# Second MoE: the second product by seven block products in passes 2 and 3, its weights' parts kept in DRAM

## The chip, the cores and the metric

The kernel runs on one core of a Trainium2 chip. The metric is device time in microseconds (us) from one execution. Before the change the median of 3 runs is 1450.73 us (1449.69 to 1453.21).

## The reference

Attention (4 batches, 8 heads, 576 tokens, head size 64, block-causal mask) gives x, 2304 tokens x 512. A first, gated MoE follows, then the second MoE, which the change is about:

```python
def _moe2_ref(x, domain_probs, w1, w2):      # x 2304x512, w1 4x512x1024, w2 4x1024x512
    p = domain_probs / (domain_probs.sum(-1, keepdims=True) + 1e-09)
    for e in range(E):                       # E = 4
        h = np.maximum(x @ w1[e], 0.0)
        out += p[:, e:e + 1] * (h @ w2[e])
```

All in fp32. On the chip each fp32 operand is split into a high and a low part of the reduced type fp32r, and a product is three matmuls: high x high, high x low, low x high.

## The kernel before, in words

Attention and the first MoE come first; the second MoE begins at about 688 us. It works in three passes (`NPASS`) of 768 tokens. A pass has two token halves t = 0, 1 of `TH` = 384 tokens. The 4 x 1024 hidden units are cut into 16 blocks q of 256, two halves a of 128 each, and taken in pairs (q0, q0+1), 8 pairs a pass.

The first product (`l1_items`) is already done with seven block products in place of eight (Winograd's form of Strassen's scheme): x and W1 are cut 2x2 into blocks, sums of blocks are formed, and seven products m = 1 to 7 are accumulated in the PSUM banks c1, c2 (two buffers each) and c3 (one). A step is one product: 6 matmuls of 128 weights x 384 columns. After a step `snap` (L923, ScalarE) saves a partial sum, or `fin` adds it (L930, VectorE) and makes h: a relu on ScalarE gives the high part (L932), a subtraction on VectorE the low one (L933), in a tile of the ring hb.

The second product (`l2_items`) is plain: for each half t and each tile of 128 tokens one PSUM bank o (three buffers) takes 12 matmuls of 128 weights (h) x 512 columns (W2), over 2 blocks, 2 halves, 3 part pairs. `tok` multiplies the bank by the expert's probability and adds it into acc (L966; L964 for the first pair), which is written out after the last pair.

Weights are loaded and prepared in every pass: `w_load` and `w2_load` on the SP queue; `w_prep` forms four sums of W1 blocks on GpSimd (L875, tile wt) and splits all into high and low parts (ScalarE and VectorE, `split3`, L811 and L814; ring w1g of 5, w1d of 1); `w2_prep` splits W2 (copy on ScalarE, low part on GpSimd, ring w2 of 3).

The order of the work: the items of the first product of a pair, with the preparation of the next pair's weights put between them, are merged by cost with the items of the second product of the pair before (`_merge`). The tile framework then orders each engine's instructions by a simulated time line, takes ready ones first, and sets all waits, so an engine's order may differ from the program's; on the chip each engine keeps that order. Weight preparation of blocks 0 and 1 runs in the last pass of the first MoE.

The first MoE serves as a comparison. Its first product has the same form with 288 columns; its split weights are made once, stored in DRAM (wcd, wod) and loaded again in later passes (L571, L578). Its second product lo writes, in its first two passes, a single PSUM bank: each part is 6 matmuls, and its result is taken out by VectorE (L783) or ScalarE (L781) before the next; 48 parts a pass.

Of the kernel before, what the change touches and what calls it, by code (L numbers as in the profile page):

```python
# [59 lines left out]
def attention_moe_moe_kernel(  # L60
# [467 lines left out]
    def w1_at(f, k):  # L528
        return wc_d[f][:, WAT[k][0] * QF:WAT[k][1] * QF].rearrange("p (h n f) -> p h n f", h=2, f=QF)
# [268 lines left out]
    if True:  # L798
# [39 lines left out]
        def w2_load(q):  # L838
            e, fo = q // QPE, (q % QPE) * QF
            r2 = p2.tile([P, 2, DM], F32, tag="wr2", name="wr2", bufs=2)  # L840
            nc.sync.dma_start(out=r2, in_=w2[e, fo:fo + QF, :].rearrange("(a p) d -> p a d", p=P))
            wq["r2", q] = r2

        def w2_prep(q):
            t = wq[q, "2"] = p2.tile([P, 2, 2, DM], F32R, tag="w2", name="w2", bufs=3)
            split3(t[:, 0], t[:, 1], wq.pop(("r2", q)), "a", "p")

        def w_prep(q):
            r = []
            d = {}  # L850

            def v(t):
                return t.rearrange("p (k f) -> p k f", f=P)

            def b(k, a):
                return d["r1"][:, k, :, a, :]

            def pair(k, src):
                t = wq[q, k] = p2r.tile([P, 2, 2, QF], F32R, tag="w1g", name="w1g", bufs=W1B)
                split3(t[:, 0], t[:, 1], src)  # L860

            def own():
# [4 lines left out]
                split3(t[:, 0].rearrange("p j (k f) -> p (j k) f", f=P),  # L867
                       t[:, 1].rearrange("p j (k f) -> p (j k) f", f=P), src)

            def sums(n):  # L870
                if n == 0:
                    d["t"] = p2r.tile([P, 4, QF], F32, tag="wt", name="wt")
                t = d["t"]
                x, y = [(b(0, 1), b(0, 0)), (b(1, 1), v(t[:, 0])), (b(1, 1), b(0, 1)), (b(1, 0), v(t[:, 1]))][n]
                nc.gpsimd.tensor_tensor(out=v(t[:, n]), in0=x, in1=y, op=ALU.subtract)  # L875

            def last():
                t = wq[q, "d"] = p2r.tile([P, 2, 1, QF], F32R, tag="w1d", name="w1d")
# [20 lines left out]
                nc.vector.tensor_tensor(out=pr_t[:, :, e], in0=pr_t[:, :, e], in1=ps_t, op=ALU.mult)  # L899

        hb = {}

        def l1_items(p, q):

            r = []
            d = {}

            def prod(m, tag, start, bufs):
                if start:
                    d[tag] = ps2.tile([P, 512], F32, tag=tag, name=tag, bufs=bufs)  # L910
                ps = d[tag][:, :TH]
                kind, n = WOP[m]
                w, x = wq[q, kind], xc[m]
                for k in range(KH):
                    ks = slice(k * P, (k + 1) * P)
                    for i, (hw, hx) in enumerate(((0, 0), (0, 1), (1, 0))):
                        mm(("p1", tag), out=ps, lhsT=w[:, hw, n, ks], rhs=x[:, hx, k],
                           start=start and k == 0 and i == 0, stop=k == KH - 1 and i == 2,
                           skip=not start)

            def snap(n):
                t = d[n] = p2.tile([P, TH], F32, tag="snap", name="snap", bufs=4)
# [31 lines left out]
        def l2_items(p, q0):  # L954
# [33 lines left out]
                            r.append((3.0 * 232, lambda t=t, tt=tt, q=q, a=a: part(t, tt, q, a)))  # L988
            return r
# [107 lines left out]
        ps2 = tc.alloc_tile_pool(name="ps2", bufs=1, space=PSUM, reuse_waits="tile")  # L1097
        for q in (0, 1):
            w2_load(q)
        prev = [(0.0, lambda q=q: w2_prep(q)) for q in (0, 1)]  # L1100
        for p in range(NPASS):
            for q0 in range(0, NQ, 2):
                last = p == NPASS - 1 and q0 == NQ - 2
                items = l1_items(p, q0) + l1_items(p, q0 + 1)
                if (p, q0) == (0, 0):
                    m = len(items) // 2
                    items = [items[m * (c == "B") + "1526743".index(x)] for c, x in
                             ("A1", "A2", "A5", "B1", "A6", "B2", "A7", "B6", "B5", "A4", "B7", "A3", "B4", "B3")]
                side = []
                if (p, q0) == (0, 0):  # L1110
                    side += wp[1][-2:]
                if not last:
                    for q in (q0 + 2, q0 + 3):
                        side.append((0.0, lambda q=q: (w_load(q % NQ), w2_load(q % NQ))))
                    for q in (q0 + 2, q0 + 3):
                        side += w_prep(q % NQ) + [(0.0, lambda q=q: w2_prep(q % NQ))]
# [12 lines left out]
        p2.release()  # L1129
# [31 lines left out]
```

## Time and profile before

| | |
|---|---|
| median of 3 runs | 1450.73 us |
| the profiled execution | 1450.08 us |
| its span, first to last instruction | 1448.1 us |
| TensorE matmul busy in the span | 1405.2 us (97%) |
| VectorE, ScalarE, GpSimd busy | 919.7, 785.9, 540.9 us |
| DMA | 229.12 MB |

The profiled execution is one run, taken by the hardware profiler. A busy time counts every moment at which at least one instruction of the engine ran; matmuls overlap, so the busy share of TensorE is not the share of its peak, and the time from one matmul's start to the next is shorter than a matmul's duration.

### The profile page before, as it was taken

The page shows a single profiled execution, that of the slowest core. Times are in us where ns is not written, and L with a number is a line of the kernel's source. Part 1 is how long each engine was busy: PE and PEld are TensorE (multiplying, and loading weights), DVE is VectorE, ACT ScalarE, POOL GpSimd, SP SyncE. Part 2 cuts the span into 40 slices and gives each one's busy share as a digit, 9 for nine tenths or more (in the row PEclk, how much of TensorE's full clock was granted, in tenths as well). Part 3 has the DMA queues.
Part 4 walks back from the last instruction along what each step waited for, and adds up shares of the span by engine and source line. Part 5 has one row for each costly group of instructions (what it writes and reads, how often), then busy time and mean ns, then how long its engine had stood idle before and what let it go on. Part 6 is the DMA issues. An engine that isn't in the chain of part 4 may idle for free. (4 is left out here: it accounts for less than half of the span.)

```text
span 1448.1 us, 23542 instructions
## 1 busy us (share of the span) xinstructions
PE 1405.2 (97%) x8288; PEld 1251.5 (86%) x8288; DVE 919.7 (64%) x1927; ACT 785.9 (54%) x1850; POOL 540.9 (37%) x562
## 2 busy tenths in 40 slices
PE   7988999899999999999999999999999999999998
PEld 3456988789888999999898999889899988899997
DVE  5778888986665546567655555765555576555553
ACT  5889988888776333443444444444444344444431
POOL 5876556631111100121433433453443344343330
PEclk9989999999999999999999999999999999999999
DMA  7797887877667987994312222332122222212201
GB/s 222 245 289 230 239 269 238 277 203 206 198 197 240 297 293 247 342 341 175 130 59 73 61 86 73 105 100 71 61 73 74 73 96 81 73 59 88 73 30 44
DMA packets 171941, 229.12 MB, mean 158 GB/s; under 512 B 70704, under 2 KB 122928, under 8 KB 171824
## 3 DMA queue, kind: packets, MB, share of 16 engines
q1 hardware_dynamic: 170736, 227.36, 48.9%
q8 instruction: 66, 1.08, 0.3%
q14 instruction: 51, 0.42, 0.1%
q10 hardware_dynamic: 1088, 0.26, 0.1%
HBM read 185.11 MB, written 42.47 MB: 157 GB/s over the span
## 5 line engine op out<-in xcount | busy, mean ns | idle before, releaser
L115 PE MATMUL o<-w,hb 128*128 128x512 f32 x1728 | 433.2, 392 | 1.0 <-ACT hb L932 1.0
L115 PEld LDWEIGHTS o<-w,hb 128*128 128x128 f32 x1728 | 321.3, 188 | 55.4 <-ACT hb L932 1.5
L115 PE MATMUL c<-xc,w1g 128*128 128x384 f32 x1728 | 342.1, 338 | 1.5 <-ACT snap L923 1.3
L115 PEld LDWEIGHTS c<-xc,w1g 128*128 128x128 f32 x1728 | 308.6, 188 | 20.8 <-ACT snap L923 2.4
L875 POOL TENSOR_TENSOR wt<-wr 128x256 f32<-128x256 f32 x96 | 90.1, 959 | 429.1 <-DMA wr<-in_moe_w_dram 392.2
L933 DVE SCALAR_TENSOR_TENSOR hb<-c,hb 128x384 fp32r<-128x384 f32 x192 | 138.8, 736 | 26.7 <-ACT hb L932 26.5
L365 POOL TENSOR_SCALAR pt<-pt,nm 128x128 f32<-128x128 f32 (+3 forms) x144 | 92.2, 646 | 170.0 <-DVE nm L362 66.2
L115 PE MATMUL lo<-g,wo 128*128 128x288 f32 x888 | 148.3, 299 | 5.1 <-DVE x L783 4.4
L932 ACT ACTIVATE hb<-c 128x384 fp32r<-128x384 f32 x192 | 96.7, 513 | 71.1 <-DVE c L930 59.7
L115 PEld LDWEIGHTS lo<-g,wo 128*128 128x128 f32 x888 | 126.2, 188 | 9.9 <-DVE x L783 6.6
L814 POOL TENSOR_TENSOR w<-wr,w 128x1024 fp32r<-128x1024 f32 x48 | 116.4, 2442 | 34.2 <-ACT w L811 32.9
L814 DVE TENSOR_TENSOR w1g<-wt,w1g 128x512 fp32r<-128x512 f32 x96 | 70.2, 733 | 88.5 <-ACT w1g L811 88.1
L923 ACT ACTIVATE snap<-c 128x384 f32<-128x384 f32 x144 | 68.3, 489 | 101.4 <-PE c L115 99.4
L811 ACT ACTIVATE w1g<-wt 128x512 fp32r<-128x512 f32 x96 | 60.6, 631 | 113.1 <-PE c L115 104.1
L966 DVE SCALAR_TENSOR_TENSOR acc<-o,pr_t,acc 128x512 f32<-128x512 f32 x126 | 92.2, 745 | 34.9 <-PE o L115 34.8
L930 DVE TENSOR_TENSOR c<-c,snap 128x384 f32<-128x384 f32 x144 | 77.1, 552 | 56.0 <-ACT snap L923 51.9
L814 DVE TENSOR_TENSOR w1g<-wr,w1g 128x512 fp32r<-128x512 f32 x48 | 37.2, 774 | 91.0 <-ACT w1g L811 91.0
L115 PE MATMUL c<-xc,wa 128*128 128x288 f32 x504 | 83.0, 300 | 2.9 <-DVE nm L361 1.8
L783 DVE TENSOR_TENSOR x<-lo,x 128x288 f32<-128x288 f32 x124 | 55.6, 452 | 42.7 <-PE lo L115 41.7
L115 PEld LDWEIGHTS c<-xc,wa 128*128 128x128 f32 x504 | 71.2, 189 | 7.1 <-DVE nm L361 2.0
L875 POOL TENSOR_TENSOR wt<-wr,wt 128x256 f32<-128x256 f32 x96 | 74.6, 777 | 3.2
L811 ACT ACTIVATE w1g<-wr 128x512 fp32r<-128x512 f32 x48 | 30.3, 630 | 80.8 <-DMA wr<-in_moe_w_dram 79.2
(142 smaller groups left out, 2435.2 us busy)
## 6 DMA issues: line engine op xcount, KB each, us to landing
wr<-in_moe_w_dram SPq DMA_DIRECT2D x96, 512.0 KB, 3.5
wa<-wcd SPq DMA_DIRECT2D x40, 512.0 KB, 5.1
wb<-wcd SPq DMA_DIRECT2D x40, 512.0 KB, 5.6
wc<-wcd SPq DMA_DIRECT2D x40, 512.0 KB, 4.3
wo<-wod SPq DMA_DIRECT2D x36, 512.0 KB, 6.4
wd<-wcd SPq DMA_DIRECT2D x40, 256.0 KB, 4.6
raw<-in_moe_w_gate_dram SPq DMA_DIRECT2D x12, 512.0 KB, 5.1
raw<-in_moe_w_val_dram SPq DMA_DIRECT2D x12, 512.0 KB, 5.5
```

Of the source, the lines that this page charges most:

```text
L115: ins = nc.tensor.matmul(out=out, lhsT=lhsT, rhs=rhs, start=start, stop=stop, skip_group_check=skip)
L365: nc.gpsimd.tensor_scalar(out=p, in0=p, scalar1=nm[:, 2 + x:3 + x], scalar2=1.0, op0=ALU.mult, op1=ALU.mult)
L783: nc.vector.tensor_tensor(out=x2[t, dm], in0=ps, in1=x2[t, dm], op=ALU.add)
L811: nc.scalar.activation(out=hi, in_=src, func=AF.Copy)
L814: (nc.vector if eng_lo == "v" else nc.gpsimd).tensor_tensor(out=lo, in0=src, in1=hi.bitcast(F32), op=ALU.subtract)
L875: nc.gpsimd.tensor_tensor(out=v(t[:, n]), in0=x, in1=y, op=ALU.subtract)
L923: nc.scalar.activation(out=t, in_=d["c1"][:, :TH], func=AF.Copy)
L930: nc.vector.tensor_tensor(out=c, in0=d[tag][:, :TH], in1=d[n], op=ALU.add)
L932: nc.scalar.activation(out=t[:, 0], in_=c, func=AF.Relu)
L933: nc.vector.scalar_tensor_tensor(out=t[:, 1], in0=c, scalar=0.0, in1=t[:, 0].bitcast(F32), op0=ALU.max, op1=ALU.subtract)
L966: nc.vector.scalar_tensor_tensor(out=acc[tt, t], in0=ps, scalar=prs["t"][:, ti, e:e + 1], in1=acc[tt, t], op0=ALU.mult, op1=ALU.add)
```

## The change

In passes 2 and 3 (index 1 and 2, `FIRSTP` = 1) the second product too is done by seven block products: h is cut into (token half, hidden half), W2 into (hidden half, output half). For each of seven products m and each of three tiles of 128 tokens, `part` makes 6 matmuls of 256 columns (two blocks q, three part pairs), and after each the half bank is added into one or two halves of acc. Nine half banks are placed in five banks (`slot`): three of tag o, two uses of c3.

For that h is kept as fp32 blocks (hf), four sums of blocks are made on GpSimd (`h_sum`), and seven operands are split (`h_split`). W2's seven split operands, sums among them, are made in pass 1 (`w2_prep`, `w2_sums`) and stored in DRAM (`w2_keep`), as W1's split parts are (`keep`); passes 2 and 3 load them (`w1_get`, `w2_get`) and prepare no weights. Pass 1 itself still computes the plain second product. The rings hb and w2 grow from 14 to 19 and from 3 to 4; hf and the sums of h use the rings wr1 and wr2.

```diff
-HB = 14
+HB = 19
+W2B = 4
+FIRSTP = 1
+        w1_d = [dram.tile([P, 14 * QF], F32, name=f"w1d{i}") for i in range(NQ)]
+        w2_d = [dram.tile([P, 7, 2, 2, QF], F32, name=f"w2d{i}") for i in range(NQ // 2)]
+        M2 = (1, 6, 2, 5, 7, 4, 3)
+        def w2_keep(q, m, t):
+            nc.sync.dma_start(out=w2_d[q // 2][:, M2.index(m), :, q % 2], in_=t.bitcast(F32))
         def w2_prep(q):
-            t = wq[q, "2"] = p2.tile([P, 2, 2, DM], F32R, tag="w2", name="w2", bufs=3)
-            split3(t[:, 0], t[:, 1], wq.pop(("r2", q)), "a", "p")
+            r = wq.pop(("r2", q))
+            t = wq[q, "2"] = p2.tile([P, 2, 2, DM], F32R, tag="w2", name="w2", bufs=W2B)
+            split3(t[:, 0], t[:, 1], r, "a", "p")
+            for m, a, n in ((1, 0, 0), (2, 1, 0), (3, 1, 1)):
+                w2_keep(q, m, t[:, :, a, n * QF:(n + 1) * QF])
+            wq["r2t", q] = r
+        def w2_sums(q):
+            r = wq.pop(("r2t", q))
+            s = p2r.tile([P, 4, QF], F32, tag="wt", name="wt")
...
+            for n, (x, y) in enumerate(((b(0, 1), b(0, 0)), (b(1, 1), s[:, 0]), (b(1, 1), b(0, 1)), (b(1, 0), s[:, 1]))):
+                nc.gpsimd.tensor_tensor(out=s[:, n], in0=x, in1=y, op=ALU.subtract)
+            t = p2.tile([P, 2, 4, QF], F32R, tag="w2", name="w2t", bufs=W2B)
+            split3(t[:, 0], t[:, 1], s, "a", "v")
+            for n, m in enumerate((5, 6, 7, 4)):
+                w2_keep(q, m, t[:, :, n])
+        def w2_get(q0, n):
+            k = min(2, 7 - 2 * n)
+            t = p2.tile([P, 2, 2, 2, QF], F32R, tag="w2", name="w2s", bufs=W2B)
+            nc.sync.dma_start(out=t[:, :k].bitcast(F32), in_=w2_d[q0 // 2][:, 2 * n:2 * n + k])
...
+        def w1_get(q):
+            for k in "abcd":
+                n = 1 if k == "d" else 2
+                t = wq[q, k] = p2r.tile([P, 2, n, QF], F32R, tag="w1d" if n == 1 else "w1g", name="w1g", bufs=1 if n == 1 else W1B)
+                nc.sync.dma_start(out=t.bitcast(F32), in_=w1_at(q, k))
+            def keep(k):
+                nc.sync.dma_start(out=w1_at(q, k), in_=wq[q, k].bitcast(F32))
...
+        def h_split(q, m, src, low=None):
+            t = hb[q, m] = p2.tile([P, 2, TH], F32R, tag="hb", name="hb", bufs=HB)
+            nc.scalar.activation(out=t[:, 0], in_=src, func=AF.Copy if low is None else AF.Relu)
+            if low is None:
+                nc.vector.tensor_tensor(out=t[:, 1], in0=src, in1=t[:, 0].bitcast(F32), op=ALU.subtract)
+            else:
+                nc.vector.scalar_tensor_tensor(
+                    out=t[:, 1], in0=src, scalar=0.0, in1=t[:, 0].bitcast(F32), op0=ALU.max, op1=ALU.subtract)
+        def h_sum(q, n, x, y, op):
...
+            nc.gpsimd.tensor_tensor(out=o, in0=x, in1=y, op=op)
+            h_split(q, {1: 5, 2: 6, 3: 7, 4: 3}[n], o)
+        def h_block(q, blk, c):
...
+            nc.scalar.activation(out=hf[q, blk], in_=c, func=AF.Relu)
+            if blk != (1, 0):
+                h_split(q, {(0, 0): 1, (0, 1): 2, (1, 1): 4}[blk], c, True)
+            if blk == (1, 0):
+                h_sum(q, 1, hf[q, (1, 0)], hf[q, (1, 1)], ALU.add)
+                h_sum(q, 2, hf[q, "s", 1], hf[q, (0, 0)], ALU.subtract)
+                h_sum(q, 3, hf[q, (0, 0)], hf[q, (1, 0)], ALU.subtract)
+            if blk == (0, 1):
+                h_sum(q, 4, hf[q, (0, 1)], hf[q, "s", 2], ALU.subtract)
+        def l2s_items(p, q0, nxt):
...
+            def slot(key, tt):
+                n, h = {("c1", 0): (0, 0), ("c1", 1): (0, 1), ("c1", 2): (1, 0), ("c2", 2): (1, 1),
+                        ("c2", 0): (2, 0), ("c2", 1): (2, 1), ("m", 0): (3, 0), ("m", 1): (3, 1), ("m", 2): (4, 0)}[key, tt]
...
+                    tag = "o" if n < 3 else "c3"
...
+            key = {1: "c1", 6: "c1", 7: "c1", 4: "c1", 2: "m", 5: "c2", 3: "c2"}
+            ADDS = {1: ((0, 0),), 2: ((0, 0),), 6: ((0, 1),), 7: ((1, 1),), 5: ((1, 1),), 4: ((1, 0),), 3: ((0, 1),)}
...
+            for x, m in enumerate(M2):
+                for tt in range(NTK):
+                    r.append((6.0 * 121, lambda m=m, tt=tt: step(m, tt)))
+                if nxt is not None and (x % 2 or x == 6):
+                    r.append((0.0, lambda x=x: w2_get(nxt, x // 2)))
...
-        prev = [(0.0, lambda q=q: w2_prep(q)) for q in (0, 1)]
+        prev = []
...
+                    else:
+                        side += [(0.0, lambda q=q: w1_get(q % NQ)) for q in (q0 + 2, q0 + 3)]
...
-                prev = l2_items(p, q0)
+                if p < FIRSTP:
+                    prev = l2_items(p, q0)
+                    if (p, q0) == (FIRSTP - 1, NQ - 2):
+                        prev += [(0.0, lambda n=n: w2_get(0, n)) for n in range(4)]
+                else:
+                    prev = l2s_items(p, q0, None if last else (q0 + 2) % NQ)
```

## Rows read from the trace of the kernel before

**Rows 1.** First line of the page: span and instructions.

```profile
span 1448.1 us, 23542 instructions
```

**Rows 2.** Stretches, about passes 1 and 2: length, busy times (instructions), clock, DMA share, GB/s.

```profile
core 0: us, PE busy (x) PEld busy (x) DVE busy (x) ACT busy (x) POOL busy (x), PEclk, DMA share, GB/s
720.00:971.00 251.00, 249.84 (x1247) 225.50 (x1246) 147.21 (x236) 111.35 (x206) 102.11 (x88) 1.00 0.25 80
971.00:1221.00 250.00, 249.81 (x1246) 225.21 (x1246) 149.74 (x238) 111.33 (x206) 99.04 (x86) 1.00 0.24 76
```

**Rows 3.** Longest wait of TensorE, 760 to 1430 us: total us, times, longest.

```profile
PE o L115 <- ACT hb L932: 1.0, 1, 1.0
```

**Rows 4.** Timeline, unbroken runs of matmuls: start us, length us, ..., count.

```profile
683.84 4.53 PE L115 MATMUL lo<-g,wo 128*128 128x288 f32 x33
688.21 7.55 PE L115 MATMUL c<-xc,w1g 128*128 128x384 f32 x42
1431.76 12.41 PE L115 MATMUL o<-w,hb 128*128 128x512 f32 x54
```

**Rows 5.** Page, costliest groups, whole run: count | busy us, mean ns | idle before.

```profile
L115 PE MATMUL o<-w,hb 128*128 128x512 f32 x1728 | 433.2, 392 | 1.0 <-ACT hb L932 1.0
L115 PE MATMUL c<-xc,w1g 128*128 128x384 f32 x1728 | 342.1, 338 | 1.5 <-ACT snap L923 1.3
L875 POOL TENSOR_TENSOR wt<-wr 128x256 f32<-128x256 f32 x96 | 90.1, 959 | 429.1 <-DMA wr<-in_moe_w_dram 392.2
L933 DVE SCALAR_TENSOR_TENSOR hb<-c,hb 128x384 fp32r<-128x384 f32 x192 | 138.8, 736 | 26.7 <-ACT hb L932 26.5
L115 PE MATMUL lo<-g,wo 128*128 128x288 f32 x888 | 148.3, 299 | 5.1 <-DVE x L783 4.4
L814 DVE TENSOR_TENSOR w1g<-wt,w1g 128x512 fp32r<-128x512 f32 x96 | 70.2, 733 | 88.5 <-ACT w1g L811 88.1
L966 DVE SCALAR_TENSOR_TENSOR acc<-o,pr_t,acc 128x512 f32<-128x512 f32 x126 | 92.2, 745 | 34.9 <-PE o L115 34.8
L930 DVE TENSOR_TENSOR c<-c,snap 128x384 f32<-128x384 f32 x144 | 77.1, 552 | 56.0 <-ACT snap L923 51.9
L783 DVE TENSOR_TENSOR x<-lo,x 128x288 f32<-128x288 f32 x124 | 55.6, 452 | 42.7 <-PE lo L115 41.7
```

**Rows 6.** First MoE, passes 1 and 2: stretches, a wait of TensorE, the adds behind lo.

```profile
149.00:341.00 192.00, 182.21 (x1309) 161.16 (x1308) 163.21 (x427) 164.41 (x457) 101.93 (x119) 1.00 0.79 247
341.00:448.00 107.00, 106.95 (x787) 95.39 (x786) 68.29 (x201) 82.43 (x234) 17.38 (x30) 1.00 0.61 182
...
PE lo L115 <- DVE x L783: 3.3, 4, 1.6
...
L783 DVE TENSOR_TENSOR x<-lo,x 128x288 f32<-128x288 f32 x40 | 18.0, 450 | 2.6 <-PE lo L115 2.2
```

**Rows 7.** Groups by line, 971 to 1221 us: a sum on GpSimd, the subtraction behind one.

```profile
L129 DVE TENSOR_TENSOR xc<-xs,xc 128x384 fp32r<-128x384 f32 x8 | 6.0, 747 | 3.5 <-ACT xc L127 3.4
L617 POOL TENSOR_TENSOR xs<-xr 128x384 f32<-128x384 f32 x2 | 2.6, 1276 | 4.6 <-issue 4.6
```

**Rows 8.** Timeline, 1016 to 1024 us: W2's split, what runs beside it.

```profile
1016.27 1.07 ACT L811 ACTIVATE w<-wr 128x1024 fp32r<-128x1024 f32 x1 [0.54 <-PE o L115]
...
1017.43 2.27 PE L115 MATMUL c<-xc,w1g 128*128 128x384 f32 x12
...
1018.57 4.76 POOL L814 TENSOR_TENSOR w<-wr,w 128x1024 fp32r<-128x1024 f32 x2
...
1021.12 2.63 DVE L933 SCALAR_TENSOR_TENSOR hb<-c,hb 128x384 fp32r<-128x384 f32 x1 [0.59 <-ACT hb L932]
```

**Rows 9.** DMA queue of 704:960, 110:300, 590:680 (packets, MB, share); then a stretch.

```profile
q1 hardware_dynamic: 15729, 21.25, 26.2%
...
q1 hardware_dynamic: 40556, 46.96, 78.4%
...
q1 hardware_dynamic: 12982, 26.82, 84.4%
...
448.00:485.00 37.00, 35.41 (x261) 34.43 (x260) 25.82 (x43) 21.07 (x44) 12.10 (x8) 1.00 0.93 313
```

More of the change, by code (lines that the diff above doesn't have):

```diff
@@ L842, in w2_load, with b, w1_at @@
             wq["r2", q] = r2
+        M2 = (1, 6, 2, 5, 7, 4, 3)
+        def w2_keep(q, m, t):
+            nc.sync.dma_start(out=w2_d[q // 2][:, M2.index(m), :, q % 2], in_=t.bitcast(F32))
         def w2_prep(q):
[L845 to L846 removed]
+            r = wq.pop(("r2", q))
[7 more added lines that the diff above has]
+            s = p2r.tile([P, 4, QF], F32, tag="wt", name="wt")
+            def b(a, n):
+                return r[:, a, n * QF:(n + 1) * QF]
+            for n, (x, y) in enumerate(((b(0, 1), b(0, 0)), (b(1, 1), s[:, 0]), (b(1, 1), b(0, 1)), (b(1, 0), s[:, 1]))):
[8 more added lines that the diff above has]
+            nc.sync.dma_start(out=t[:, :k].bitcast(F32), in_=w2_d[q0 // 2][:, 2 * n:2 * n + k])
+            for x in range(k):
+                wq[q0, "2", M2[2 * n + x]] = t[:, x]
+        def w1_get(q):
[3 more added lines that the diff above has]
+                nc.sync.dma_start(out=t.bitcast(F32), in_=w1_at(q, k))
+        def w1_at(q, k):
+            return w1_d[q][:, WAT[k][0] * QF:WAT[k][1] * QF].rearrange("p (h n f) -> p h n f", h=2, f=QF)
         def w_prep(q):
@@ L901, in attention_moe_moe_kernel @@
         hb = {}
+        hf = {}
+        def h_split(q, m, src, low=None):
[7 more added lines that the diff above has]
+        def h_sum(q, n, x, y, op):
+            if n in (1, 3):
+                hf[q, "u", n] = p2.tile([P, 2, DM], F32, tag="wr2", name="hs", bufs=2).rearrange("p a d -> p (a d)")
+            o = hf[q, "s", n] = hf[q, "u", n - (n + 1) % 2][:, (n + 1) % 2 * TH:((n + 1) % 2 + 1) * TH]
+            nc.gpsimd.tensor_tensor(out=o, in0=x, in1=y, op=op)
+            h_split(q, {1: 5, 2: 6, 3: 7, 4: 3}[n], o)
+        def h_block(q, blk, c):
+            t, a = blk
+            if a == t:
+                hf[q, "t", t] = p2r.tile([P, NKT, QF], F32, tag="wr1", name="hf", bufs=2).rearrange("p a d -> p (a d)")
+            hf[q, blk] = hf[q, "t", t][:, a * TH:(a + 1) * TH]
+            nc.scalar.activation(out=hf[q, blk], in_=c, func=AF.Relu)
[7 more added lines that the diff above has]
+                h_sum(q, 4, hf[q, (0, 1)], hf[q, "s", 2], ALU.subtract)
         def l1_items(p, q):
@@ L988, in l2_items, with add, done, part @@
                             r.append((3.0 * 232, lambda t=t, tt=tt, q=q, a=a: part(t, tt, q, a)))
+            return r
+        begun = set()
+        def l2s_items(p, q0, nxt):
+            r = []
+            e = q0 // QPE
+            NTK = TH // P
+            bank = {}
+            opened = {}
+            def slot(key, tt):
+                n, h = {("c1", 0): (0, 0), ("c1", 1): (0, 1), ("c1", 2): (1, 0), ("c2", 2): (1, 1),
+                        ("c2", 0): (2, 0), ("c2", 1): (2, 1), ("m", 0): (3, 0), ("m", 1): (3, 1), ("m", 2): (4, 0)}[key, tt]
+                new = n not in bank
+                if new:
+                    tag = "o" if n < 3 else "c3"
+                    bank[n] = ps2.tile([P, 512], F32, tag=tag, name=tag, bufs=3 if n < 3 else 1)
+                return bank[n][:, h * QF:(h + 1) * QF], new, n
+            def add(t, n, tt, ps):
+                ti = (p * TP + t * TH) // P + tt
+                pr = prs["t"][:, ti, e:e + 1]
+                if q0 == 0 and (p, tt, t) not in begun:
+                    begun.add((p, tt, t))
+                    acc[tt, t] = p2.tile([P, DM], F32, tag=f"acc{t}{tt}", name="acc")
+                o = acc[tt, t][:, n * QF:(n + 1) * QF]
+                if q0 == 0 and (p, tt, t, n) not in begun:
+                    begun.add((p, tt, t, n))
+                    nc.vector.tensor_scalar(out=o, in0=ps, scalar1=pr, scalar2=None, op0=ALU.mult)
+                else:
+                    nc.vector.scalar_tensor_tensor(out=o, in0=ps, scalar=pr, in1=o, op0=ALU.mult, op1=ALU.add)
+            def done(t, tt):
+                if q0 + 2 == NQ:
+                    ti = (p * TP + t * TH) // P + tt
+                    nc.sync.dma_start(out=out[ti * P:(ti + 1) * P, :], in_=acc[tt, t])
+            key = {1: "c1", 6: "c1", 7: "c1", 4: "c1", 2: "m", 5: "c2", 3: "c2"}
+            ADDS = {1: ((0, 0),), 2: ((0, 0),), 6: ((0, 1),), 7: ((1, 1),), 5: ((1, 1),), 4: ((1, 0),), 3: ((0, 1),)}
+            def part(m, tt):
+                k = key[m]
+                ps, new, n = slot(k, tt)
+                ts_ = slice(tt * P, (tt + 1) * P)
+                for x, q in enumerate((q0, q0 + 1)):
+                    h, w = hb[q, m], wq[q0, "2", m]
+                    for i, (hh, hw) in enumerate(((0, 0), (0, 1), (1, 0))):
+                        first = x == 0 and i == 0
+                        if first and m in (1, 2, 5) and not new:
+                            last_mm["p2", k, tt] = opened[n]
+                        mm(("p2", k, tt), out=ps, lhsT=h[:, hh, ts_], rhs=w[:, hw, x],
+                           start=first and new, stop=x == 1 and i == 2, skip=not new)
+                        if first and new:
+                            opened[n] = last_mm["p2", k, tt]
+                return ps
+            def step(m, tt):
+                ps = part(m, tt)
+                for t, n in ADDS[m]:
+                    add(t, n, tt, ps)
+                if m == 4:
+                    done(1, tt)
+                if m == 3:
+                    done(0, tt)
+            for x, m in enumerate(M2):
[3 more added lines that the diff above has]
+                    r.append((0.0, lambda x=x: w2_get(nxt, x // 2)))
@@ L1111, in attention_moe_moe_kernel @@
                     side += wp[1][-2:]
+                if (p, q0) == (0, 0):
+                    for q in (0, 1):
+                        side += [(0.0, lambda q=q: w2_prep(q)), (0.0, lambda q=q: w2_sums(q))]
                 if not last:
[L1113 to L1116, printed above, removed]
+                    if p < FIRSTP and q0 + 2 < NQ:
+                        for q in (q0 + 2, q0 + 3):
+                            side.append((0.0, lambda q=q: (w_load(q % NQ), w2_load(q % NQ))))
+                        for q in (q0 + 2, q0 + 3):
+                            side += w_prep(q % NQ) + [(0.0, lambda q=q: w2_prep(q % NQ)), (0.0, lambda q=q: w2_sums(q))]
+                    else:
+                        side += [(0.0, lambda q=q: w1_get(q % NQ)) for q in (q0 + 2, q0 + 3)]
                 n = len(items)
```

7 lines of the change are left out of this document (added).

## Prediction

> **What bounds the kernel now.** I read the page first, then the busy times stretch by stretch. The profiled execution took 1450.08 us, of which the span is 1448.1 [rows 1]; the median of the runs shown is 1450.73, so a time worked out against the profiled one needs 0.65 added, which is below what I can resolve. The change lies in the second MoE, which runs from 688 us to the end. There TensorE has next to no gap: in passes 1 and 2 it is busy 249.8 of 251 and of 250 us, at the full granted clock, while VectorE is at 59 to 60%, ScalarE at 44%, GpSimd at 40% and the DMA engines at 24 to 25% [rows 2]. From 760 to 1430 us its longest wait behind another engine is 1.0 us in all [rows 3]. So a pass lasts as long as its matmuls take to issue, and the question is what a matmul costs. A pair of weight blocks (q0, q0+1) has 84 matmuls of the first product (14 steps of 6, 384 columns) and 72 of the second (512 columns), 156 in all; the 1246 instructions of pass 2 are eight pairs, 31.25 us each [rows 2].
>
> The rate of issue is read from unbroken runs, less the last one's duration. 288 columns: (4.53 - 0.30)/32 = 0.132 us. 384: (7.55 - 0.34)/41 = 0.176. 512: (12.41 - 0.39)/53 = 0.227 [rows 4, 5]. Check: 84 x 0.1759 + 72 x 0.2268 = 14.78 + 16.33 = 31.1 us a pair, against 31.25 seen.
>
> **The change, part by part.**
>
> *The second product, passes 2 and 3* (16 pairs). Out go 16 x 72 = 1152 matmuls of 512 columns: 1152 x 0.2268 = 261.3 us. In come 16 x 7 products x 3 token tiles x 2 blocks x 3 = 2016 of 256 columns. No unbroken run of 256 columns with full weights is in the trace. Above, one costs no more than a 288-column one, 0.132 us; below, no less than half a 512-column one, 0.1134 (a fixed part can't be negative). So the product costs 229 to 266 us: from 33 us won to 5 us lost. At 2.4 GHz the columns alone take 0.120, 0.160 and 0.213 us, so the three rows leave 12, 16 and 13 ns of fixed cost; with 13 ns a 256-column matmul takes 0.120 us. The nearest row, 288 columns, less 32 columns gives 0.119. I take 0.120: 2016 x 0.120 = 241.9 us, **19.4 us won**, 1.2 us a pair.
>
> The Trainium skill speaks against short matmuls here: "TensorE: Matmul & The Clock Gate" has a weight load of 128 columns at about 107 ns (section "LDWEIGHTS (loading the stationary operand)") and says that it overlaps a running matmul only in another row group (section "The mechanism"). By it a 512-column matmul would issue every 213 + 107 = 320 ns and a 256-column one every 214, and the change would lose 2016 x 0.214 - 1152 x 0.320 = 63 us. The 0.227 us row disagrees: of such a load only 13 ns shows; the measurement decides.
>
> *Handing banks to VectorE.* Today a pair ends 6 accumulations in one of three o banks, each 12 matmuls (2.7 us) long. After, 21 parts of 6 matmuls (0.72 us) each need an add before TensorE may go on in that place; the parts share five banks, and the third product takes the c3 bank twice a pair, which the first product uses too. That is 16 x 21 = 336 handovers. The nearest rows are those of the first MoE, where the product lo lives in a single bank and each part is 6 matmuls: in its first pass, with VectorE 85% busy (163.21 of 192 us), 48 such parts cost 3.3 us of waiting, 0.07 us each; in its second pass, with VectorE at 64%, TensorE is busy 106.95 of 107 us [rows 6]. So 0 to 23 us. VectorE's load per pair: out go 6 adds (4.5 us), the weight splits (2 x 3.5 x 0.733 = 5.1) and 8 hb subtractions (5.9), in come 21 adds of 256 columns, 6 hb subtractions (4.4) and 8 subtractions behind a GpSimd sum (8 x 0.747 = 6.0) [rows 5, 7]. A 256-column add: L783 and L930, the same operation at 288 and 384 columns, differ by 100 ns, 1.04 ns a column; 745 - 256 x 1.04 = 0.48 us, 10.1 for 21. Net +5.0: from 18.7 to 23.7 us of 30, 79%, between the two rows. But lo's parts follow one another in one bank, while here two thirds have another bank's part between them, and 14 first-product steps a pair can be put in the gaps. I take 0.02 us: **6.7 us lost**.
>
> The Trainium skill ("PSUM — Partial Sum Buffer", section "PSUM bank collisions raise a hardware error") wants a bank guarded whole, not by address. No row here shows two accumulations in one bank. By it the second token tile of a product can't start before the add of the first is done, as they share a bank (rival 3).
>
> *h in blocks.* Per pair ScalarE gets 22 passes over 128x384 for 8, and loses ten weight copies: about even at 44%, nothing on the path. GpSimd gets 8 sums of at most 1.28 us (10.2 us) [rows 7] and loses all weight work (8 sums near 0.87, two splits of 2.4: 11.8 us) [rows 5, 8]. A split of 2.4 us can hold up VectorE's subtraction for as long: L933 took 2.63 us beside one [rows 8]; that pause shortens to 1.3. The chain relu, sum, sum, copy, subtract (some 4.5 us) makes product 6 ready later than hb today; the next pair's first product covers it, 14.8 us that needs none of it. Nothing, except in the last pair.
>
> *Loads in passes 2 and 3.* A pair reads two sets of split W1 (1.84 MB each) and 3.67 MB of split W2: 7.3 MB in 30 us, 245 GB/s, where it was 76. The first MoE moved 298 GB/s from 590 to 680 us at 84% of the engines [rows 9]. All are issued on SP; behind one that waits for its buffer the other loads stand. They have half a pair (15 us) or more in hand. I cost it at nothing; uncovered, a 1 MB load at that rate is 3.5 us a pair, 56 in all.
>
> *Pass 1.* Here W2's sums and all parts are made and stored. Per pair GpSimd gets 8 sums (7 us, to 63%), ScalarE 2 copies of 1.07 us, VectorE 2 subtractions near 1.5 us: all beside TensorE's 31.25 us. The DMA is the tight part. Stored are 14 x 1.84 MB of W1 (the first two blocks mostly before 700 us) and 16 x 1.84 of W2: 55 MB; loads of 14 blocks, 14.7 MB; the two W1 sets for pass 2, 3.7; x and output, 3.2. 77 MB in 251 us is 306 GB/s. While engines are busy they move 21.25/(0.262 x 256) = 317 GB/s in this pass today, 315 from 110 to 300 us, where much is stores, 353 from 590 to 680 [rows 9]: 87 to 97% of the pass. From 448 to 485 us they were at 93% and TensorE lost 1.6 of 37 us [rows 9]; all of that for 251 us would be 10.8, the 84% stretch gives 0. I take **3 us lost**; worst at the 247 GB/s of 149 to 341 us [rows 6]: 77/0.247 = 312 us, 61 lost.
>
> W2's split now waits for the end of the second product with only 4 buffers, two of them for the sums. Before, both splits waited for it too, and TensorE issued 12 first-product matmuls meanwhile [rows 8]; the same covers it here.
>
> *Pass 1 to 2, and the end.* The first four loads of kept W2 follow the last old product: some 5 us behind first-product steps, 0.5 lost. At the end, 54 x 0.2268 = 12.2 us of second product came after the last first-product matmul [rows 4]; now, if 27 of 126 can go ahead, 99 x 0.120 = 11.9, with handovers that nothing fills: 1 lost. **1.5 lost.**
>
> Sum: 1450.1 - 19.4 + 6.7 + 3 + 1.5 = **1442 us**.
>
> **Rivals.**
> 1. *All handovers hidden*, as in the first MoE's second pass, and the stores too: 1450.1 - 19.4 - 0 = 1431. For it: the first product's steps as filler. Against: VectorE fuller.
> 2. *Pass 1 becomes a DMA pass* (the slower side). Stores fill the engines, the weight loads land late behind them on the same queue, and TensorE waits for W1. It decides when pass 1 grows by more than the other 11 us won: below 77/(0.251 + 0.011) = 294 GB/s. At 277 GB/s, between the 298 and the 247 seen, 27 us more: 1442 - 3 + 27 = 1466. For it: no stretch of 90 us moved over 298 here. Against: none was asked to.
> 3. *Adds set the pace of the second product*: a third of the parts, 7 a pair, follow a part in their own bank; where 0.48 us of add is never filled that is 16 x 7 x 0.48 = 54 us, at half 27: 1442 - 6.7 + 27 = 1462. For it: VectorE at 79%; against: fillers.
> 4. *A wash*: handovers at 0.04 us (13 us), pass 1 at 5: about 1450.
>
> **Numbers.** Forecast 0.40, rival 1 0.17, rival 2 0.17, rival 3 0.09, rival 4 0.17. 0.3% (4.4 us) is about what a measurement of this kernel tells from no change: faster 0.57, same 0.17, slower 0.26. The forecast's own range is 1436 to 1446. Range 1428 to 1463: it takes in 0.119 us a matmul with nothing lost, and rival 3.
>
> **What would show it.** Second-product runs of 256 columns at 0.120 us; passes 2 and 3 near 241 us each against 250; waits of the second product behind the adds of about 7 us; pass 1 near 254 us with the DMA share above 0.85. I am wrong if those runs issue at over 0.130, if waits behind adds pass 20 us, or if pass 1 passes 265 us.

## The result, and the profile after

| | before | after |
|---|---|---|
| median of 5 runs | 1450.73 us (1448.90 to 1453.68) | 1429.70 us (1427.74 to 1432.97) |
| ratio of after to before | | 0.9854, 95% interval 0.9832 to 0.9876 |
| the profiled execution | 1450.08 us | 1431.91 us |
| first matmul of the second MoE | 688.2 us | 692.1 us |
| from there to the last matmul of the plain second product of pass 1 | 261.6 us | 262.3 us |
| from there to the end (passes 2 and 3) | 498.3 us | 475.6 us |

The kernel is 21.0 us faster; 1442 was forecast, with 1428 to 1463 as range. So the sign was right and the size less than half of what came; the time is that of rival 1 (1431). The stages, read from the starts of matmuls in the two traces: pass 1 cost 0.7 us, passes 2 and 3 won 22.6. The 3.9 us by which the second MoE starts later lie in the part that wasn't changed; a later profile of the same kernel (e12) starts it at 688.1. Without that part the second MoE takes 759.9 us in the trace before and 738.0 in the trace after.

The first line of the page of the kernel after:

```profile
span 1430.1 us, 26340 instructions
```

The view of stretches of the kernel after, against [rows 2] (columns as there):

```profile
720.00:971.00 251.00, 248.68 (x1252) 225.64 (x1253) 167.73 (x246) 120.34 (x220) 137.34 (x139) 1.00 0.90 311
971.00:1221.00 250.00, 249.40 (x1763) 248.61 (x1762) 180.14 (x361) 113.46 (x251) 79.85 (x75) 1.00 0.71 252
```

TensorE has still no gap to speak of, now with 1763 instructions in 250 us. The matmuls got shorter, not the gaps smaller. VectorE went from 60 to 72% in pass 2, not to the 79% reckoned; the DMA engines are 90% busy in pass 1 and move 311 GB/s.

An unbroken run of the second product in the timeline of the kernel after (start, length, count):

```profile
1408.34 5.07 PE L117 MATMUL o<-w2s,hb 128*128 128x256 f32 x41
```

The groups by line of the kernel after, from 971 to 1221 us (busy, mean ns), to set beside [rows 4, 5, 7]:

```profile
L117 PE MATMUL o<-w2s,hb 128*128 128x256 f32 x909 | 130.0, 282 | 0.5 <-DVE acc L1106 0.5
L1106 DVE SCALAR_TENSOR_TENSOR acc<-o,pr_t,acc 128x256 f32<-128x256 f32 x133 | 62.3, 478 | 28.4 <-PE o L117 26.7
L957 DVE TENSOR_TENSOR hb<-hs,hb 128x384 fp32r<-128x384 f32 x68 | 45.6, 687 | 2.5 <-ACT hb L955 2.4
L959 DVE SCALAR_TENSOR_TENSOR hb<-c,hb 128x384 fp32r<-128x384 f32 x51 | 29.8, 584 | 5.7 <-ACT hb L955 5.5
```

(5.07 - 0.28)/40 = 0.120 us from start to start: the forecast value. The add takes 0.478 us (0.48 forecast).

The view of waits of the kernel after has two lines for TensorE from 965 us on (total us, times, longest); the handovers to VectorE cost 1.1 us, not 6.7:

```profile
PE c L117 <- DMA w1g<-w1d: 1.5, 1, 1.5
PE o L117 <- DVE acc L1106: 1.1, 2, 0.6
```

From start to start these two waits behind an add cost 1.4 us: the view leaves out the end of the running matmuls. Each part has one add, into one half of acc (not "one or two"). How the handovers come to cost so little is seen in the timeline of pass 2 (start, length; TensorE's matmuls and the adds alone):

```profile
1064.37 0.87 PE L117 MATMUL o<-w2s,hb 128*128 128x256 f32 x6
1065.07 1.04 PE L117 MATMUL c<-xc,w1g 128*128 128x384 f32 x5
1065.28 0.48 DVE L1106 SCALAR_TENSOR_TENSOR acc<-o,pr_t,acc 128x256 f32<-128x256 f32 x1 [0.57 <-PE o L117]
1065.95 0.87 PE L117 MATMUL c<-w2s,hb 128*128 128x256 f32 x6
1066.66 1.04 PE L117 MATMUL c<-xc,w1g 128*128 128x384 f32 x5
1066.86 0.48 DVE L1106 SCALAR_TENSOR_TENSOR acc<-c,pr_t,acc 128x256 f32<-128x256 f32 x1 [0.64 <-PE c L117]
1067.54 0.87 PE L117 MATMUL o<-w2s,hb 128*128 128x256 f32 x6
1068.25 0.51 PE L117 MATMUL c<-xc,w1g 128*128 128x384 f32 x2
```

Behind each part of 6 matmuls stand 5 matmuls of the first product, 0.88 us from start to start; the add runs beneath them (1065.28 to 1065.76) and is done before the next part starts. The framework's order mixes the products by single matmuls, not by steps of 6.

### The profile page after: what moved, and what is told of

Same layout as the page of the kernel before. It is cut to its first block, busy times and chain, and to the rows that moved or that the text cites. A ratio compares the mean times of both kernels' runs of the same rounds, so it can differ in the third digit from the quotient of the medians.

```text
span 1430.1 us, 26340 instructions
## 1 busy us (share of the span) xinstructions
PE 1381.3 (97%) x9152; PEld 1276.4 (89%) x9152; DVE 995.2 (70%) x2151; ACT 791.6 (55%) x1930; POOL 546.6 (38%) x594
## 4 chain that ended last, share of the span: by engine, by line
PE 77%; DVE 6%; DMA 6%; ACT 5%; POOL 3%; issue 3%; SPq 1%; DVEq 0%; ACTq 0%; POOLq 0%
PE c L117 34%; PE o L117 24%; PE lo L117 6%; PE s L117 4%; PE obank L117 3%; PE t L117 2%; DMA raw<-in_moe_w_gate_dram 1%; PE tbank L389 1%; DMA raw<-in_moe_w_out_dram 1%; PE s L308 1%; ACT pt L339 1%; DVE raw L508 1%; DMA wr<-in_moe_w_dram 1%; DVE nm L337 1%; DMA w1g<-w1d 1%
## 5 line engine op out<-in xcount | busy, mean ns | idle before, releaser
L117 PE MATMUL o<-w2s,hb 128*128 128x256 f32 x1728 | 243.5, 282 | 1.1 <-DVE acc L1106 1.1
L117 PEld LDWEIGHTS o<-w2s,hb 128*128 128x128 f32 x1728 | 231.8, 189 | 2.0 <-DVE acc L1106 1.7
L966 POOL TENSOR_TENSOR hs<-hf 128x384 f32<-128x384 f32 x64 | 64.1, 1023 | 287.4 <-ACT hf L974 256.3
L1106 DVE SCALAR_TENSOR_TENSOR acc<-o,pr_t,acc 128x256 f32<-128x256 f32 x264 | 123.4, 478 | 57.8 <-PE o L117 55.3
L117 PE MATMUL o<-w,hb 128*128 128x512 f32 x576 | 142.6, 392 | 1.8 <-ACT hb L1016 1.2
L974 ACT ACTIVATE hf<-c 128x384 f32<-128x384 f32 x128 | 65.7, 513 | 116.1 <-DVE c L1011 58.4
L117 PEld LDWEIGHTS o<-w,hb 128*128 128x128 f32 x576 | 107.1, 188 | 21.8 <-ACT hb L1016 1.9
L957 DVE TENSOR_TENSOR hb<-hs,hb 128x384 fp32r<-128x384 f32 x128 | 87.0, 694 | 5.5 <-ACT hb L955 5.3
L117 PE MATMUL c<-xc,wc 128*128 128x288 f32 x432 | 72.2, 302 | 1.8 <-ACT snap L709 1.7
L339 ACT ACTIVATE pt<-s,nm 128x128 f32<-128x128 f32 (+3 forms) x128 | 67.5, 529 | 9.5 <-DVE nm L337 4.9
```

The lines of the kernel that those rows point to most:

```text
L117: ins = nc.tensor.matmul(out=out, lhsT=lhsT, rhs=rhs, start=start, stop=stop, skip_group_check=skip)
L339: nc.scalar.activation(out=pt[:, x * nk:(x + 1) * nk], in_=sp[:, x - x0], func=AF.Exp, bias=nm[:, x:x + 1], scale=1.0, accum_out=nm[:, 2 + ...
L957: nc.vector.tensor_tensor(out=t[:, 1], in0=src, in1=t[:, 0].bitcast(F32), op=ALU.subtract)
L966: nc.gpsimd.tensor_tensor(out=o, in0=x, in1=y, op=op)
L974: nc.scalar.activation(out=hf[q, blk], in_=c, func=AF.Relu)
L1106: nc.vector.scalar_tensor_tensor(out=o, in0=ps, scalar=pr, in1=o, op0=ALU.mult, op1=ALU.add)
```

## The experiments

Theory A: the second product costs the issue of its matmuls, and the handovers are free because the framework's order fills them. Theory B: they are free in any order. Theory C: part of the gain is relief of the other engines from weight work. Theory D: pass 1 stayed under the limit of the DMA, but close to it. Against A stood the prediction's rival 3 (VectorE sets the price). Times are medians, of 8 runs for e1 and e11, of 4 for e2, e9 and e12, of 2 for the others; where a time is set against "before", that is the kernel before on the same chip.

**e1: W1 kept alone.** The second product plain in every pass; only W1's parts are kept, and W2 is loaded and split in every pass.

```diff
+SECOND = 3
-                if p >= FIRSTP:
+                if p >= SECOND:
...
-                if p < FIRSTP:
+                if p < SECOND:
```

> W1's split parts are kept in DRAM and loaded in passes 2 and 3, as after the change; the second product stays plain in all passes, W2 is loaded and split in every pass. Theory A (only the number and length of the second product's matmuls matters): the same matmuls as before, so 1450 us, within 3. Theory C (part of the gain is relief: no weight sums and fewer splits on VectorE, ScalarE and GpSimd in passes 2 and 3): VectorE and GpSimd get 5 and 7 us a pair lighter, and 3 to 10 us of the 21 come already here: 1441 to 1447.

Measured 1446.46 us against 1451.24, ratio 0.998 (0.9963 to 0.9998): 0.3 to 5.4 us faster. In the same stretches as [rows 2] TensorE is busy without a gap:

```profile
720.00:971.00 251.00, 251.00 (x1255) 227.01 (x1254) 139.16 (x225) 104.42 (x194) 87.90 (x72) 1.00 0.55 190
971.00:1221.00 250.00, 250.00 (x1251) 226.13 (x1250) 110.58 (x174) 77.40 (x142) 44.80 (x22) 1.00 0.50 160
```

With the same matmuls 8 and 5 more fit into the two stretches, some 1.6 and 1.0 us. So a small part of the gain comes without the block products, a term the prediction had at nothing; C calls it relief, but e1 also has the larger rings hb and w2, and no run parts the two.

**e2: the block products in pass 3 alone** (as e1 with `SECOND = 2`, all stores of the change in pass 1).

> The block products only in pass 3; pass 2 has the plain second product with W1 from DRAM and W2 split anew; pass 1 as after the change (all stores). Theory A: 8 of the 16 pairs, half of the 22.6 us that passes 2 and 3 won: 11 us less than before, 1439 to 1440. If pass 1's stores or the step from one pass to the next carry a price, or the gain sits in one of the passes, it is away from half by 3 us or more.

Measured 1439.86 us, 11.4 less than before: half, as A says. The interval (9 to 14 us less) leaves room for some 2 us: beyond that, pass 1's stores and the step between passes carry no price of their own.

**e4: the parts together.** From pass 2 on each matmul is tied behind the one before it in the program's order, and the parts follow three first-product steps.

```diff
+        if fixed["on"]:
+            if fixed["last"] is not None:
+                tc.add_manual_dep(ins.ins, fixed["last"].ins.name, NOSYNC, reason="in the order given")
+            fixed["last"] = ins
...
-                _merge(items, prev)
+                fixed["on"] = p >= FIRSTP
+                if p > FIRSTP or (p == FIRSTP and q0):
...
+                    run(items[:steps[2] + 1] + prev + items[steps[2] + 1:])
```

> From pass 2 on TensorE keeps the order as written, and a pair's 21 parts of the second product stand together behind three steps of the first product, so no first-product matmul stands between two parts. Theory A (the handovers to VectorE cost nothing because first-product matmuls fill them): the 7 parts a pair that follow a part in their own bank wait for an add, 0.48 us and two signals, some 0.7 us each, 16 x 7 x 0.7 = 78 us: about 1505, waits of TensorE behind the adds of 60 us or more. Theory B (no filler is needed, the parts in other banks and a quick add are enough): under 10 us of waits, 1430 to 1440.

Measured 1650.67 us. The view of waits of this kernel, TensorE's longest from 965 us on:

```profile
PE o L118 <- DVE acc L1111: 66.7, 88, 2.9
PE c L118 <- ACT snap L1009: 48.0, 60, 1.5
PE c L118 <- DVE acc L1111: 18.5, 32, 0.6
PE o L118 <- DVE acc L1109: 5.7, 8, 1.2
```

A stretch of its timeline (matmuls and adds alone):

```profile
1107.71 0.97 PE L118 MATMUL c<-w2s,hb 128*128 128x256 f32 x6 [0.58 <-DVE acc L1111]
1108.73 0.48 DVE L1111 SCALAR_TENSOR_TENSOR acc<-c,pr_t,acc 128x256 f32<-128x256 f32 x1 [1.07 <-PE c L118]
1109.27 0.98 PE L118 MATMUL c<-w2s,hb 128*128 128x256 f32 x6 [0.58 <-DVE acc L1111]
```

128 waits behind adds, 8 a pair. A part that waits starts 1.56 us after the one before it (1107.71, 1109.27) in place of 0.72: a handover with nothing in the gap costs 0.84 us, of which the view of waits shows 0.58; the rest is the end of the running matmuls and the start of the next. That is 128 x 0.84 = 107 us (112 when every such gap of the trace is added up, since some are longer), and the waits of the first product behind its snap come on top, 58 us counted in the same way, since it has lost its filler too. Some 36 us of the 221 lie in gaps too short for the view. B falls. My 1505 counted the second product's waits alone.

**e5: whole steps, merged as the program has them** (e4's tie, `_merge` kept).

> From pass 2 on TensorE keeps the order in which the program merges the two products (a step of the first product, one or two parts of the second, and so on), in place of the order made by the framework, which mixes single matmuls. Theory A in its strict form (the fine mixing is needed): one gap in three between parts has no filler and a third of these are in one bank, 2 to 3 waits of 0.7 us a pair, 16 x 2.5 x 0.7 = 28 us: about 1457. If whole steps are filler enough: 1430 to 1435. Theory B: 1430 to 1435.

Measured 1577.07 us: both figures missed, in A's direction. The view of waits of this kernel, TensorE's from 965 us on:

```profile
PE o L118 <- DVE acc L1111: 77.0, 88, 3.9
PE c L118 <- DVE acc L1111: 14.1, 17, 0.9
PE o L118 <- DVE acc L1109: 10.0, 8, 4.3
```

A stretch of its timeline (matmuls and adds alone):

```profile
1105.49 0.87 PE L118 MATMUL o<-w2s,hb 128*128 128x256 f32 x6
1106.40 0.48 DVE L1111 SCALAR_TENSOR_TENSOR acc<-o,pr_t,acc 128x256 f32<-128x256 f32 x1 [0.42 <-PE o L118]
1106.93 0.99 PE L118 MATMUL o<-w2s,hb 128*128 128x256 f32 x6 [0.58 <-DVE acc L1111]
1107.76 1.21 PE L118 MATMUL c<-xc,w1g 128*128 128x384 f32 x6
```

113 waits, 7 a pair: in this order the two parts without a step between them are each time token tiles 0 and 1, which share a bank; I had taken one in three. Where VectorE is behind other work the wait grows, to 4 us.

**e8: the same order, the half banks dealt otherwise.**

```diff
-                n, h = {("c1", 0): (0, 0), ("c1", 1): (0, 1), ("c1", 2): (1, 0), ("c2", 2): (1, 1),
-                        ("c2", 0): (2, 0), ("c2", 1): (2, 1), ("m", 0): (3, 0), ("m", 1): (3, 1), ("m", 2): (4, 0)}[key, tt]
+                n, h = {("c1", 0): (0, 0), ("c1", 1): (1, 0), ("c1", 2): (0, 1), ("c2", 1): (1, 1),
+                        ("c2", 0): (2, 0), ("c2", 2): (2, 1), ("m", 0): (3, 0), ("m", 1): (3, 1), ("m", 2): (4, 0)}[key, tt]
```

> As e5_order_as_merged, but the half banks are dealt otherwise: token tile 1 of the products goes to another bank than token tile 0, which stands directly before it. If a part waits because the add reads the other half of its bank (theory A, by bank): the 7 waits a pair of e5 fall to 1 or 2 (the third product in c3 keeps its own), 20 to 40 us of the 147 stay: 1450 to 1470. If VectorE is simply late (whatever the bank) or the chain of products waits: 1560 to 1580 as e5.

Measured 1482.82 us: 94 us of e5's 147 gone by a bank number. The view of waits of this kernel, TensorE's behind the adds of L1111 from 690 us on, against 88 and 17 times in e5:

```profile
PE c L118 <- DVE acc L1111: 13.9, 17, 0.9
PE o L118 <- DVE acc L1111: 2.8, 4, 1.2
```

What is left is mainly the third product in c3, one wait a pair, as expected. The wait in e5 is for the other half of the bank, whose columns the waiting part doesn't touch. This is what the Trainium skill asks of programs in "PSUM — Partial Sum Buffer", section "PSUM bank collisions raise a hardware error" (guard by bank, not by address); the runs show the framework's waits, not a collision. Of the 53 us left, some 14 lie before the end of pass 1's second product, where the tied order holds too: that stage takes 282 us for 262, but 36 more first-product matmuls (6 us) stand in it.

**e3, e10, e11: more load on VectorE.** Before 14 (e3) or 7 (e10, `tt < 1`) of a pair's 21 adds VectorE reads the half bank once more; e11 is e3 with e8's banks.

```diff
+                if tt < 2:
+                    nc.vector.tensor_reduce(out=prs["x"], in_=ps, axis=AX.X, op=ALU.max)
```

> The changed kernel, and before 14 of a pair's 21 adds VectorE reads the same half bank once more (a maximum over it, some 0.42 us): 5.9 us a pair, 94 us in all, VectorE from 72 to 91% in pass 2. Theory A (the fine order fills the handovers, whatever VectorE's load below full): waits of TensorE behind VectorE stay under 5 us, 1430 to 1437. The prediction's rival (VectorE's load sets the price of a handover, 0.07 us at 85%): 336 x 0.07 = 24 us more, 1454 or above.

> Half the dose of e3: one more read before 7 of a pair's 21 adds, 2.9 us a pair, 47 us in all; VectorE from 72 to about 80% in passes 2 and 3, the load that the prediction had reckoned with. If the price of a handover is a straight line in the load, half of e3's 42 us: 1450. If there is a knee (the order fills all up to some load): under 8 us, 1430 to 1438. The prediction's 0.02 us a handover stands for 7 us: 1437.

> e3's full dose (14 more reads a pair) with the half banks dealt as in e8. If e3's 42 us are waits for the other half of a part's own bank, most goes: 1435 to 1450. If VectorE is simply too late at that load, whatever the bank: 1465 to 1475 as e3.

Measured 1434.86 (e10), 1472.11 (e3), 1453.78 (e11). The stretch from 980 to 1180 us (columns as in [rows 2]), of the kernel after:

```profile
980.00:1180.00 200.00, 199.40 (x1407) 198.61 (x1406) 142.65 (x286) 89.48 (x198) 62.62 (x59) 1.00 0.71 252
```

The same stretch of e10:

```profile
980.00:1180.00 200.00, 197.96 (x1393) 196.61 (x1391) 158.71 (x328) 88.15 (x196) 63.82 (x57) 1.00 0.73 249
```

The same stretch of e3:

```profile
980.00:1180.00 200.00, 194.69 (x1321) 189.89 (x1320) 164.05 (x356) 78.84 (x178) 58.63 (x51) 0.99 0.68 232
```

The same stretch of e11:

```profile
980.00:1180.00 200.00, 195.38 (x1347) 192.28 (x1346) 165.29 (x361) 82.91 (x187) 59.99 (x52) 0.99 0.70 240
```

The views of waits of e3, TensorE's behind the adds of L1109 from 965 us on:

```profile
PE o L117 <- DVE acc L1109: 15.2, 26, 2.0
PE c L117 <- DVE acc L1109: 3.4, 14, 0.9
```

The same of e11:

```profile
PE o L117 <- DVE acc L1109: 8.9, 8, 2.8
PE c L117 <- DVE acc L1109: 4.4, 14, 1.9
```

VectorE is busy 71, 79, 82 and 83% of the stretch. That share is an outcome: a pair that waits lasts longer. Per pair (210 matmuls) VectorE works 21.3, 23.9, 26.1 and 25.8 us, which is 71, 80, 87 and 86% of the 29.85 us that a pair of the changed kernel lasts in this stretch. From 71 to 80% the time grows by 5 to 7 us, little more than the spread of the runs, from 80 to 87% by 37 to 40: a knee between the two. A in its strict form (any load below full) falls, and rival 3 is a real mechanism: the change stays short of it. Some 18 us of e3's 43 go with the banks (e3 ran on another chip than e10 to e12; set against before on the same chip it is 21). They are waits for the other half bank, 26 waits in o against 8; as e8's dealing still leaves 3 of 21 parts behind a neighbour in their own bank (7 before), some such waits may be in the rest. What else the rest is, e3 doesn't part: the extra read loads VectorE, but it also holds its half bank 0.42 us longer before the add, at any load. And 15 of e3's 43 us lie in gaps too short for the view of waits.

**e6: half the columns.**

```diff
-                o = acc[tt, t][:, n * QF:(n + 1) * QF]
+                    nc.gpsimd.memset(acc[tt, t], 0.0)
+                o, ps = acc[tt, t][:, n * QF:n * QF + P], ps[:, :P]
...
-                        mm(("p2", k, tt), out=ps, lhsT=h[:, hh, ts_], rhs=w[:, hw, x],
+                        mm(("p2", k, tt), out=ps[:, :P], lhsT=h[:, hh, ts_], rhs=w[:, hw, x, :P],
```

> The second product's matmuls in passes 2 and 3 take only the first 128 of their 256 columns (half of those outputs is left out and set to zero). If an issue costs the columns and 13 ns: 0.066 us each, 2016 x (0.120 - 0.066) = 109 us less than the changed kernel, 1321. If a weight load sets a floor near that of the 128-column transposes of the attention (about 0.109 us from start to start): 22 us less, 1408. The lower the floor, the more a shorter block could still win.

Measured 1420.14 us (1416.27 and 1424.02), 8 to 10 below the change in place of 109; the adds are half as wide too. An unbroken run of 18 in the timeline of this kernel, between two of the first product (TensorE's matmuls alone, the slower of the two runs):

```profile
1286.09 2.67 PE L117 MATMUL c<-xc,w1g 128*128 128x384 f32 x14
1288.60 2.12 PE L117 MATMUL o<-w2s,hb 128*128 128x128 f32 x18
1290.55 2.15 PE L117 MATMUL c<-xc,w1g 128*128 128x384 f32 x11
```

Its group by line, from 971 to 1221 us:

```profile
L117 PE MATMUL o<-w2s,hb 128*128 128x128 f32 x899 | 118.3, 276 | 0.4 <-DVE hb L957 0.4
```

By itself the run gives (2.12 - 0.28)/17 = 0.108 us. But the 14 first-product matmuls in front take 2.51 us, 0.05 more than 14 x 0.1755: the first of them, which stands behind half-column ones, takes 0.23 us in place of 0.175, and the first half-column one 0.06. Both runs together give (4.46 - 14 x 0.1755)/18 = 0.111 us: half the columns, and only 0.009 us less. Below some 235 columns, an estimate ((0.111 - 0.013) us at 2.4 GHz, 0.013 being what 0.120 us has over 256 columns), something other than the columns sets the pace. It is close to the 107 ns which the Trainium skill gives for a load of 128 columns ("TensorE: Matmul & The Clock Gate", section "LDWEIGHTS (loading the stationary operand)"); that it overlaps a running matmul only in another row group (section "The mechanism") no run here bears out. That the weight load is the floor is likely, but no run parts it from another fixed cost.

At this pace 2016 x 0.009 = 18 us are to be won, near the 22 expected for the floor. The profiled run gave some 8 of them back at a lower clock. After TensorE had idled 1.3 of the 4 us from 1168 to 1172, the view of stretches shows a granted clock of 0.52 in the next 17 us, so the lower level of 1.2 GHz for nearly all of them, with TensorE busy throughout (17 x 0.48 = 8 us):

```profile
1172.00:1189.00 17.00, 17.00 (x75) 17.00 (x75) 7.88 (x19) 4.29 (x9) 2.52 (x3) 0.52 0.39 141
```

The other run, 1416.27, is 13 below the change.

**e7: W2's parts stored twice in pass 1.**

```diff
+            nc.sync.dma_start(out=w2_e[q // 2][:, M2.index(m), :, q % 2], in_=t.bitcast(F32))
```

> Pass 1 stores each of W2's parts a second time, to a tensor that nobody reads: 29.4 MB more in the pass, which moves 78 MB in 251 us at 90% of the DMA engines after the change. Theory D (pass 1 was close to being bound by the DMA; room for 10% or 9 MB): at the 345 GB/s that full engines give, 107 MB take 311 us, some 55 us more: 1475 to 1490. If stores only wait in the queue and nobody waits for them: under 10 us more, 1430 to 1440.

Measured 1486.53 us. The view of DMA queues from 704 to 960 us (packets, MB, share), of the kernel after:

```profile
q1 hardware_dynamic: 52726, 79.21, 89.9%
```

The same view of the kernel with the doubled stores:

```profile
q1 hardware_dynamic: 72677, 90.18, 101.3%
```

The view of stretches of that kernel:

```profile
720.00:971.00 251.00, 223.98 (x1033) 191.42 (x1031) 139.98 (x194) 96.44 (x172) 120.01 (x122) 0.96 1.01 352
```

Full engines carry 352 GB/s with this mix of loads and stores, and TensorE then idles: pass 1 takes 300.6 us for 262.3. D holds: the change uses 79.21/(0.352 x 256) = 88% of that, near the share of 89.9%. Passes 2 and 3, where nothing changes, took 19 us more as well. Counted by matmuls from the start of the second MoE, and not by that boundary, TensorE is 49 us behind the changed kernel at the last plain matmul of pass 1 (991 us; 48 first-product matmuls, 8 us, have moved behind it), 57 at 1028 us, and 1 more at the end. Two more stretches of this kernel show why: the engines are full until about 1015 us, and after 1025 TensorE has no gap and the full clock again.

```profile
1005.00:1015.00 10.00, 6.23 (x32) 4.88 (x30) 5.50 (x8) 5.11 (x11) 6.49 (x6) 1.00 1.03 401
1025.00:1050.00 25.00, 25.00 (x179) 25.00 (x178) 18.68 (x38) 11.88 (x27) 7.71 (x8) 1.00 0.65 208
```

**e9, e12: e8's banks in the framework's order, beside the change itself.**

> The changed kernel in the framework's own order, with the half banks dealt as in e8: neighbouring parts never share a bank, the third product's apart. With 1.1 us of waits behind adds left there is nothing to win: 1427 to 1433, as the changed kernel. If waits too short for the view of waits are still paid, up to 5 us less: 1423 to 1427.

> The changed kernel itself, as the measure for the three others on the same chip: 1428 to 1433.

Measured 1429.91 and 1427.74 us, ratios to before 0.9847 (0.9814 to 0.9880) and 0.9841 (0.9816 to 0.9867): no difference. With the gaps filled the banks' dealing is worth nothing measurable. (It doesn't part all neighbours, as I had expected: token tile 2 of products 1 and 7 stands before tile 0 of products 6 and 4 in the same bank, so 3 parts a pair still follow one in their own bank, for 7.) No version that does the whole work beats the change.

## Why the prediction fell short

- *Handovers, 6.7 us lost*: this step failed, by size. It measured 1.1 us of waits, 1.4 from start to start. I priced a handover from the first MoE's single bank with VectorE at 85%, by a share of parts that have a neighbour in another bank. What decides is whether matmuls that need nothing stand in the gap (e4: 0.84 us each without, e5) and whether VectorE's work and its hold on a bank stay below a knee (e3, e10). My 79% for VectorE was too high by 7 points, 2.2 us a pair. 0.9 of them: L933's subtraction, 0.736 us before, takes 0.584 (L959) now that the splits of 2.4 us on GpSimd are gone (in pass 2 before, the 8 of 64 that ran beside one took 2.16 us on average, the 52 beside nothing 0.55). Another 0.5: the 8 subtractions behind a GpSimd sum take 0.687, not 0.747. Most of the rest: I added single durations, and neighbours on VectorE overlap at their ends (in pass 2 196 us of durations in 180 us busy, 160 in 150 before).
- *Issue rate, 19.4 us won*: right by pace, 0.120 us forecast and measured, but 2 us too small. For the plain product I took the best run, 0.227 us. From start to start, added up over passes 2 and 3, its 1152 matmuls took 265.0 us in the trace before (0.230 each, switches to the first product and short stalls included), the 2016 new ones 243.6 after (0.121 each, the waits behind adds included): 21.4 won.
- *Pass 1, 3 us lost*: 0.7 measured. The worry was real but the ceiling is 352 GB/s at least (e7), the upper of the rates I had (353), not the 317 of mixed stretches.
- *Transition and end, 1.5 us lost*: TensorE waits 1.5 us once for a load of W1 at 961 us (0.5 in e12's trace); the end shows one wait of 0.6. The size came out, but by luck: I had the first W2 loads at the start, and pass 2's start had gaps of 1.2 us before too.
- *Relief, nothing*: 0.3 to 5.4 us by e1; not in my sum. It isn't on top of the row on issue: in e1's trace the 1152 plain matmuls take 263.7 us, so 1.3 of the 3.7 us that they took beyond my 261.3 go with it.

So the second product won 21.4 us and the first product's matmuls in passes 2 and 3 another 1.0 (229.0 to 228.0): 22.4 of the 22.6. All three losses I put in were biased the same way, and their sum of 11 us was half the gain. The measured time lies in my range by its lower end, which was built on nothing lost. Rival 1's mechanism (handovers and stores hidden) is what the runs show; that its 1431 is so close is in part luck: it leaves out 2 us more at the second product's matmuls and 1 at the first's, and 0.7 lost in pass 1.

## What to carry to other kernels

Where TensorE is full, count its instructions: the gain of a change that shortens them is that count, the old ones at their average in the trace, the new ones at the rate of unbroken runs, as long as other matmuls that need nothing can stand in each new gap and the engine that empties PSUM stays below its knee (here between 80 and 87% of a pair's time, with reads that also held the banks longer). Reckon that load as work per unit of the undisturbed time; the busy share of a run that already waits hides it. The order is worth more than the arithmetic won: the same instructions cost 1430, 1577 or 1651 us. And two accumulations in one bank wait for one another under this framework's scheduling: part them by bank wherever nothing fills the gap.

## What the runs showed of the hardware that was not expected

With its own 128x128 weights for each, a matmul of 128 columns issues every 0.111 us, one of 256 every 0.120, one of 288 every 0.132: from 256 to 128 columns a shorter moving operand buys 0.009 us (e6). Behind a run of such short matmuls the first of 384 columns takes 0.23 us in place of 0.175, so a short run read by itself looks quicker than it is.

The 16 DMA engines carried loads beside stores, W2's in rows of 1 KB, at 352 GB/s when full (e7, 90.18 MB in 72677 packets, 1.2 KB each), as much as the 353 of a stretch of mostly loads [rows 9]. That is no fixed ceiling: right after, from 985 to 1015 us, full engines moved 399 GB/s in packets of 2.6 KB, mostly loads (the view of DMA queues of e7: packets, MB, share):

```profile
q1 hardware_dynamic: 4651, 11.97, 103.1%
```
